# Reordering the opening of a one-core FFT filter and maxout MoE kernel: filter copies, a sine table, products, one x load, and the last transposes

## The chip, the cores and the metric

The kernel runs on one core of one Trainium2 chip. The metric is the device time of one execution in microseconds (us), as the median of several; lower is better. The core has five engines that matter here: TensorE (PE in the profile; its weight loads are PEld), VectorE (DVE), ScalarE (ACT), GpSimd (POOL) and SyncE (SP). SP does nothing but issue DMA transfers; POOL issues some too. All transfers are carried by the core's 16 DMA engines.

## The reference

The input x has 8 batches of 3072 rows with 256 columns. Along the 3072 rows each batch is filtered in the frequency domain; then every row goes through a maxout layer.

```
X = np.fft.rfft(x, axis=1)                  # x: 8 x 3072 x 256
Y = X * (filt_r + 1j * filt_i)[None]        # filter: 1537 x 256
y = np.fft.irfft(Y, n=3072, axis=1)
g = np.maximum(y @ w1, y @ w2)              # w1, w2: 256 x 1024
out = g @ w_out                             # w_out: 1024 x 256
```

## The kernel before

**The factorization.** The transform over 3072 = 96 × 32 points is done as matrix products with small tables of sines. Stage 1 transforms over 96 points (table C1), stage 2 over the 32 that are left, with one table per frequency group (U, made of arguments `ua` by a Sin on ScalarE in two halves, `sines_u(0)` and `sines_u(1)`, L247 on); then the product with the filter F; stage 3 goes back over 32 (tables VP and VQ, which `table_v` and `put_v` make out of U, L256 to L280); stage 4 goes back over 96 (table G1, made by `table_g`, L251). The maxout is written as relu(y (w1 − w2)) w_out + y M with M = w2 w_out, so the weights are prepared once: Wd = w1 − w2 by `prep_wd`, M by `prep_t` and `prep_m`.

**The steady part.** Batches 1 to 7 pass through DRAM between the stages. The main loop has 64 tiles `tt` of 384 rows, each with 8 steps: `moe_h` (y times Wd, L482) and `moe_o` (the second product with Wo, L536, of the tile before). Between them the stages of the following batches are slotted in: two lists, `todo` and `mid`, name the step at which a piece of work is put. The order of instructions on every engine is the order of the program text; each engine runs its own list in order and waits by semaphores where it needs another's result or a buffer.

**The opening.** Batch 0 is done on the chip without DRAM, before the first tile, and this is where the change lies. In order:

- `s1t(c)` and `t1(n)` (L554 to L575): stage 1 and transposes into bt[0]. ScalarE and VectorE evict alternately.
- `s2(0, v)` (L379), v = 0 to 5: four groups of columns each, half s = 0 in one PSUM tile and s = 1 in another, `px`.
- `products(v)` (L657): for each half one `product` (L388) of 128 × 1024 elements with the filter. VectorE reads px from PSUM. GpSimd does the half s = 1 of v in `POOLED` = (0, 2, 3, 4), out of a copy in SBUF that ScalarE makes in `stage_x(v)` (L650); for v = 5 `shared_product` (L394) splits that half between both.
- `s3t(v)` (L577): one matmul on a table of ones as a filler (L581; two for v = 1), then 32 matmuls in pairs (L587), and evictions into the tile zT, one per g, by ScalarE (L597), or for v >= 4 and g = 1 by VectorE (L595).
- `t2(c)` (L599): transposes of a piece of zT into zr[0] (L608), evicted by VectorE or ScalarE or both.
- `s4(tt)` (L454): stage 4 for one tile, y evicted by ScalarE and VectorE.

**The filter.** F has 128 partitions: in each half g of 64, the first 32 are loaded from DRAM by GpSimd (`load_f`, L111, 16 partitions per transfer), and the other 32 are a copy of them. The copies are made by `double_f` (L124): the columns w 0 to 8 by VectorE (four `tensor_copy`, one for each g and each of real and imaginary part, L128) and w 8 to 12 by four transfers that SyncE issues (L130). `fix_f` then sets one row. Stage v reads columns 2v and 2v + 1.

**Around it in the queues.** SyncE's list has the four copies of F, then the four loads of w1 and w2 into WS (`load_w`). GpSimd's list, behind the filter loads, has: the product of v = 0, the load of batch 1's first x (`load_x(1, 0, 2)`, 384 KB, L89), the products of v = 2, 3, 4, its share of v = 5, `load_x(1, 2, 2)`, `load_wo` (w_out into Wo, L294), one `prep_wd`, two more x loads, and the rest of the preparation. On TensorE, behind the last s3t, stand `f1(1, 0)`, a filler (`spin`), `t2(0)`, `f1(1, 1)`, a filler, `s4(0)`, `f1(1, 2)`, `f1(1, 3)`, and the main loop. `f1` (L323) is stage 1 of batch 1: one matmul of x with C1 (L330) into a PSUM tile `pa`, and at once its eviction to `at`. The PSUM pool `ps` has six buffers, `pso` two.

Of the kernel before, what the change touches and what calls it, by code (L numbers as in the profile page):

```python
# [15 lines left out]
D = 256  # L16
# [11 lines left out]
def kernel(  # L28
# [95 lines left out]
    def double_f(h, g, ri, engine):  # L124
        w0, w1 = WP[h]
        o_, i_ = F[64 * g + 32:64 * g + 64, ri, w0:w1], F[64 * g:64 * g + 32, ri, w0:w1]
        if engine is V:
            V.tensor_copy(o_, i_)  # L128
        else:
            nc.sync.dma_start(out=o_, in_=i_)  # L130
# [25 lines left out]

    hv = init.tile([128, 2, 1], FP32)
# [22 lines left out]
    def table_c():  # L180
# [10 lines left out]
        S.activation(C1, uc.rearrange("p k r -> p (k r)"), AF.Sin, bias=zero[0:NP], scale=TWO_PI)  # L191

# [58 lines left out]
    def table_g():  # L251
        pg = ps.tile([96, NP], FP32, tag="ps", name="pg")
        TE.matmul(pg, C1, I128[0:NP, 0:NP], start=True, stop=True)
# [68 lines left out]

    def f1(b, c, engine):  # L323
        if c == 0:
# [3 lines left out]
        at = at_[b]  # L328
        pa = ps.tile([96, 2, D], FP32, tag="ps", name="pa")
        TE.matmul(pa, C1, xb[b, c // 2][:, 2 * (c % 2):2 * (c % 2) + 2], start=True, stop=True)  # L330
# [57 lines left out]
    def product(E, v, s, px, pool=None):  # L388
# [3 lines left out]
        return pq  # L392

    def shared_product(v, s, px, xs_, pool):  # L394
        pq = pool.tile([128, 2, 2, D], BF16, tag="pq", name="pq")
        V.tensor_tensor(pq[:, 0], px, F[:, 0, 2 * v:2 * v + 2, s], OP.mult)
        V.tensor_tensor(pq[:, 1, 0], px[:, 0], F[:, 1, 2 * v, s], OP.mult)
        G.tensor_tensor(pq[:, 1, 1], xs_[:, 1], F[:, 1, 2 * v + 1, s], OP.mult)
# [178 lines left out]
    def s3t(v, pq):  # L577
        pool, tag = (ps, "ps") if v % 2 else (pso, "po")
        pz = [pool.tile([128, 2, 2, 2, 2, NM], FP32, tag=tag, name="pt%d" % g) for g in range(2)]
        for _ in range(2 if v == 1 else 1):  # L580
            TE.matmul(pz[0].rearrange("p i s r c m -> p (i s r c m)"), W1[:, 0:128], W1, start=True, stop=True)  # L581
        for i in range(2):
            for s in range(2):
                for dc in range(2):
                    for q, tab in enumerate((VP, VQ)):
                        for g in range(2):
                            TE.matmul(pz[g][:, i, s, :, dc], pq[s][64 * g:64 * g + 64, q, i, 128 * dc:128 * dc + 128],  # L587
                                      tab[64 * g:64 * g + 64, 2 * v + i, s].rearrange("p (r m) -> p r m", r=2),
                                      start=(q == 0), stop=(q == 1))
        zv = zT.rearrange("p c m (w g) q -> p w g (c m) q", g=2)  # L590
        for g in range(2):
            o_ = zv[:, 2 * v:2 * v + 2, g]
            i_ = pz[g].rearrange("p i s r c m -> p i (c m) (s r)")
            if v >= 4 and g == 1:
                V.tensor_copy(o_, i_)  # L595
            else:
# [232 lines left out]
```

## Time and profile before

| what | value |
| --- | --- |
| three runs | 498.36, 496.78, 498.27 us (median 498.27) |
| the profiled execution | 498.64 us, its span 496.8 us |
| TensorE busy, share of the span | 483.8 us, 97% |
| VectorE, ScalarE, GpSimd busy | 335.4, 320.4, 258.7 us (68%, 64%, 52%) |
| mean granted clock of TensorE | 0.989 |
| stretch 21.30 to 24.70 us: TensorE busy, granted clock | 1.39 us, 0.50 |
| stretch 31.50 to 35.00 us: TensorE busy, granted clock | 3.50 us, 1.00 |
| first matmul of the main loop (L482) | begins at 37.73 us |

The span runs from the first to the last instruction in the trace. Only the slices of the first 40 us have TensorE below nine tenths. A line of the chain of waits has a start, a length and an instruction; a line of the timeline has start, length, engine, source line, operation, output and inputs by the program's names, shapes and count, and in brackets the idle time before it with the engine that ended it. A line of transfers has the name, the queue, the count, the size and the median time from issue to landing in us. A granted clock of 0.50 is half of TensorE's full clock.

### The profile page before, as it was taken

Reading aid. Unit: us, or ns where it says so; the run is one execution under the profiler, and the core shown is the slowest. Engines: PE = TensorE matmul, PEld = TensorE weight load, DVE = VectorE, ACT = ScalarE, POOL = GpSimd, SP = SyncE. Lnnn points to the kernel's source line nnn. Section 1 sums busy time; section 2 is a strip of 40 time slices with the busy share of each in tenths; the row PEclk is TensorE's granted clock in tenths of the full one; section 3 lists DMA queues with packets and bytes.
Section 4 is the critical chain, followed back from the end, with each engine's and each line's share of the span. In section 5 each row is a group of like instructions: output and inputs, shape, how many; then the busy total and the mean of one; then the engine's idle time right before and its main releaser. Section 6 shows DMA issues by size and latency. Waiting matters only on the chain.

```text
span 496.8 us, 14137 instructions
## 1 busy us (share of the span) xinstructions
PE 483.8 (97%) x5759; PEld 353.5 (71%) x5759; DVE 335.4 (68%) x535; ACT 320.4 (64%) x667; POOL 258.7 (52%) x342
## 2 busy tenths in 40 slices
PE   7699999999999999999999999999999999999997
PEld 3457777777777777777777777776777777777775
DVE  7886788468855688467855688457873688556542
ACT  5777478667775677576866668665766656464442
POOL 8694868318466594528646295536842212222220
PEclk9879999999999999999999999999999999999999
DMA  8989988996789867896789977897776834531112
GB/s 128 161 242 224 259 269 260 284 234 190 204 266 221 216 210 223 249 225 174 231 257 227 183 244 211 257 215 168 227 231 175 181 104 129 157 120 66 64 64 86
DMA packets 76626, 97.30 MB, mean 196 GB/s; under 512 B 7985, under 2 KB 54354, under 8 KB 75186
## 3 DMA queue, kind: packets, MB, share of 16 engines
q1 hardware_dynamic: 63218, 66.71, 52.1%
q0 software_dynamic: 13200, 29.60, 21.4%
q8 instruction: 45, 0.74, 0.7%
q14 instruction: 19, 0.16, 0.1%
q10 hardware_dynamic: 144, 0.09, 0.1%
HBM read 53.87 MB, written 47.19 MB: 203 GB/s over the span
## 4 chain that ended last, share of the span: by engine, by line
PE 92%; DMA 3%; ACT 2%; POOL 1%; issue 1%; DVE 0%; SPq 0%; POOLq 0%
PE po L536 34%; PE ph L482 33%; PE po L534 8%; PE pz L408 5%; PE pc L443 3%; PE px L384 2%; PE pa L355 2%; DMA xb<-in_x_dram 2%; DMA zr<-zd 1%; PE pt L587 1%; DMA zd<-zt 1%; PE pr L608 1%; POOL xb L89 1%; PE pt L581 1%; PE pa L330 1%
## 5 line engine op out<-in xcount | busy, mean ns | idle before, releaser
L486 ACT ACTIVATE gt<-ph 128x384 bf16<-128x384 f32 x357 | 175.7, 496 | 138.8 <-PE ph L482 136.2
L536 PE MATMUL po<-Wo,gt 128*128 128x256 bf16 x1528 | 262.7, 273 | 1.2 <-issue 1.2
L536 PEld LDWEIGHTS <-gt 128*128 128x128 bf16 x1528 | 144.7, 98 | 68.1 <-issue 13.5
L495 POOL DMA_DIRECT2D out_dram<-ot x186 | 103.1, 558 | 154.7 <-DVE ot L547 138.7
L390 DVE TENSOR_TENSOR pq<-px,F 128x1024 bf16<-128x1024 f32 x91 | 106.9, 1218 | 25.7 <-PE px L384 25.4
L484 DVE TENSOR_SCALAR gt<-ph 128x384 bf16<-128x384 f32 x155 | 83.6, 551 | 53.5 <-PE ph L482 47.1
L482 PEld LDWEIGHTS <-Wd 128*128 128x128 bf16 x1024 | 99.6, 98 | 13.7 <-issue 0.3
L104 POOL TENSOR_TENSOR xb<-XF 128x512 bf16<-128x512 f32 x48 | 61.3, 1277 | 66.9 <-DMA XF<-in_x_dram 31.7
L547 DVE TENSOR_SCALAR ot<-po 128x512 f32<-128x512 f32 x83 | 57.0, 686 | 35.0 <-PE po L536 33.1
L105 POOL TENSOR_TENSOR xb<-XF 128x512 bf16<-128x512 f32 x48 | 61.1, 1274 | 0.0
L359 ACT ACTIVATE at<-pa 128x512 bf16<-128x512 f32 x96 | 51.8, 611 | 3.4 <-PE pa L355 3.3
L412 ACT ACTIVATE zt<-pz 128x512 bf16<-128x512 f32 x84 | 45.6, 594 | 5.7 <-PE pz L408 1.9
L448 ACT ACTIVATE ce<-pc 128x384 f32<-128x384 f32 x56 | 23.7, 490 | 6.7 <-PE pc L443 6.0
L408 PE MATMUL pz<-pq,VP 64*64 64x256 bf16 x336 | 22.2, 281 | 0.0
L384 PE MATMUL px<-bt,U 64*64 64x256 bf16 x384 | 20.4, 283 | 1.2 <-ACT VQ L279 0.7
L408 PE MATMUL pz<-pq,VQ 64*64 64x256 bf16 x336 | 21.1, 269 | 0.0
L408 PEld LDWEIGHTS <-VP 64*64 64x64 bf16 x336 | 10.0, 105 | 13.3 <-issue 12.7
L355 PE MATMUL pa<-xb,CT 64*64 64x512 bf16 x192 | 18.0, 377 | 0.0
L443 PEld LDWEIGHTS <-zr 48*128 48x128 bf16 x896 | 13.1, 93 | 4.8 <-issue 4.4
L443 PE MATMUL pc<-G,zr 48*128 48x48 bf16 x896 | 15.4, 180 | 0.3 <-DMA zr<-zd 0.3
L384 PEld LDWEIGHTS <-U 64*64 64x64 bf16 x384 | 10.6, 109 | 3.9 <-issue 3.6
L618 PE MATMUL pd<-W 128*128 128x512 bf16 x28 | 9.2, 437 | 1.5 <-DVE zero L150 1.5
(383 smaller groups left out, 632.1 us busy)
## 6 DMA issues: line engine op xcount, KB each, us to landing
out_dram<-ot POOLq DMA_DIRECT2D x186, 128.0 KB, 3.8
XF<-in_x_dram SPq DMA_DIRECT2D x96, 192.0 KB
ad<-at SPq DMA_DIRECT2D x56, 192.0 KB
zd<-zt SPq DMA_DIRECT2D x42, 256.0 KB
zr<-zd SPq DMA_DIRECT2D x56, 192.0 KB
bt<-ad SPq DMA_DIRECT2D x13, 768.0 KB
WS<-in_moe_w_dram SPq DMA_DIRECT2D x4, 512.0 KB
xb<-in_x_dram POOLq DMA_DIRECT2D x8, 192.0 KB, 5.6
```

The lines of the kernel that those rows point to most:

```text
L104: G.tensor_tensor(t_[:, 0], f[:, 0], f[:, 1], OP.add)
L105: G.tensor_tensor(t_[:, 1], f[:, 0], f[:, 1], OP.subtract)
L359: S.activation(at[:, m0:m0 + 2], pa[g], AF.Copy)
L390: E.tensor_tensor(pq, px.rearrange("p (o i) d -> p o i d", o=1).to_broadcast([128, 2, 2, D]), F[:, :, 2 * v:2 * v + 2, s], OP.mult)
L408: TE.matmul(pz[g][64 * s:64 * s + 64, i], tab[64 * g:64 * g + 64, 2 * v + i, s], pq[s][64 * g:64 * g + 64, q, i], start=(q == 0), stop=(q ...
L412: S.activation(zt[:, :, g], pz[g], AF.Copy)
L482: TE.matmul(ph, Wd[:, dc, 128 * j:128 * j + 128], y_[:, dc], start=(dc == 0), stop=(dc == 1))
L484: V.tensor_scalar(gt[tt][:, j], ph, 0.0, None, OP.max)
L486: S.activation(gt[tt][:, j], ph, AF.Relu)
L495: E.dma_start(out=dst, in_=ot[tt // 2][:, 3 * (tt % 2) + c])
L536: TE.matmul(p_, g_[:, n - 2, blk], Wo[:, n - 2], start=(e == 0), stop=(e == 9))
L547: V.tensor_scalar(ot[tt // 2][:, e - 1:e + 1], po[q // 2 % 2], SCALE, None, OP.mult)
```

## The change

All of it is in the opening.

- `double_f` takes a range of columns. SyncE copies w 4 to 8 of g = 1 (two transfers) and then w 8 to 12 of both g (four), six transfers instead of four. VectorE copies w 0 to 8 of g = 0 and w 0 to 4 of g = 1.
- `sines_u(1)` is put ahead of the t1 loop; it stood behind `stage_x(2)`. `table_v(1, 0)` follows `table_v(0, 0)`; `put_v(1, 0)` and `table_v(1, 1)` with its `put_v` stand one place earlier too.
- `shared_product` goes. GpSimd takes half s = 1 of v = 0, 2, 3 and 5 whole; VectorE takes both halves of v = 1 and 4. `stage_x(4)` is no longer needed.
- `load_x(1, 0, 2)` is issued behind the product of v = 3, GpSimd's third; it stood behind the first.
- zT has another order of its dimensions: rows in eight groups `o` of four first, partitions of the transposed piece as (g, w, q). To match, G1 is made from a second sine table, CP, whose columns have that order. For v = 5 the eviction is in two parts, the first of the eight groups alone and then the seven others, so that `t2(0)`, which reads the first group, depends on the first part.
- `f1` is split into `f1_in` (the matmul) and `f1_out` (the eviction and, every second time, the store). The matmuls of `f1(1, 0 to 3)` stay near t2(0) and s4(0); the evictions come behind s4(0), the last two in step 0 of the main loop. The fillers write one tile `pd` of the pool pso, and there are two more of them behind s4(0).

```diff
@@ -121,8 +121,7 @@
                     o_ = F[64 * g + r0:64 * g + r0 + 16, ri, w0:w1].rearrange("p w s d -> p (w s) d")
                     G.dma_start(out=o_[:, n0:n], in_=src)
 
-    def double_f(h, g, ri, engine):
-        w0, w1 = WP[h]
+    def double_f(w0, w1, g, ri, engine):
         o_, i_ = F[64 * g + 32:64 * g + 64, ri, w0:w1], F[64 * g:64 * g + 32, ri, w0:w1]
         if engine is V:
             V.tensor_copy(o_, i_)
@@ -154,6 +153,7 @@
     jb = init.tile([128, 16], FP32)
     cid = init.tile([128, 128], FP32)
 
+    CP = init.tile([NP, 96], BF16)
     hv = init.tile([128, 2, 1], FP32)
     load_x(0, 0, 1)
     G.iota(pid, pattern=[[1, 1]], base=0, channel_multiplier=1, allow_small_or_imprecise_dtypes=True)
@@ -189,6 +189,8 @@
         V.tensor_scalar(rc, uc, RND, RND, OP.add, OP.subtract)
         V.tensor_tensor(uc, uc, rc, OP.subtract)
         S.activation(C1, uc.rearrange("p k r -> p (k r)"), AF.Sin, bias=zero[0:NP], scale=TWO_PI)
+        S.activation(CP.rearrange("p (g w c) -> p g w c", g=2, c=4),
+                     uc.rearrange("p (w g s) r -> p g w (s r)", g=2, s=2), AF.Sin, bias=zero[0:NP], scale=TWO_PI)
 
     def table_ct():
         G.memset(CT, 0.0)
@@ -250,7 +252,7 @@
 
     def table_g():
         pg = ps.tile([96, NP], FP32, tag="ps", name="pg")
-        TE.matmul(pg, C1, I128[0:NP, 0:NP], start=True, stop=True)
+        TE.matmul(pg, CP, I128[0:NP, 0:NP], start=True, stop=True)
         S.activation(G1, pg, AF.Copy)
 
     def table_v(h, q):
@@ -320,14 +322,22 @@
     zd = {}
     at_ = {}
 
+    pas = {}
+
     def f1(b, c, engine):
+        f1_in(b, c)
+        f1_out(b, c, engine)
+
+    def f1_in(b, c):
+        pas[c] = ps.tile([96, 2, D], FP32, tag="ps", name="pa")
+        TE.matmul(pas[c], C1, xb[b, c // 2][:, 2 * (c % 2):2 * (c % 2) + 2], start=True, stop=True)
+
+    def f1_out(b, c, engine):
         if c == 0:
             ad[b] = dram.tile([96, NM, D], BF16, tag="ad", name="ad")
         if c % 4 == 0:
             at_[b] = apool.tile([128, 8, D], BF16, tag="at", name="at")
-        at = at_[b]
-        pa = ps.tile([96, 2, D], FP32, tag="ps", name="pa")
-        TE.matmul(pa, C1, xb[b, c // 2][:, 2 * (c % 2):2 * (c % 2) + 2], start=True, stop=True)
+        at, pa = at_[b], pas.pop(c)
         o_ = at[0:96, 2 * (c % 4):2 * (c % 4) + 2]
         if engine is V:
             V.tensor_copy(o_, pa)
@@ -389,13 +399,6 @@
         pq = (pool or pqpool).tile([128, 2, 2, D], BF16, tag="pq", name="pq")
         E.tensor_tensor(pq, px.rearrange("p (o i) d -> p o i d", o=1).to_broadcast([128, 2, 2, D]),
                         F[:, :, 2 * v:2 * v + 2, s], OP.mult)
-        return pq
-
-    def shared_product(v, s, px, xs_, pool):
-        pq = pool.tile([128, 2, 2, D], BF16, tag="pq", name="pq")
-        V.tensor_tensor(pq[:, 0], px, F[:, 0, 2 * v:2 * v + 2, s], OP.mult)
-        V.tensor_tensor(pq[:, 1, 0], px[:, 0], F[:, 1, 2 * v, s], OP.mult)
-        G.tensor_tensor(pq[:, 1, 1], xs_[:, 1], F[:, 1, 2 * v + 1, s], OP.mult)
         return pq
 
     def s3(b, v, pq):
@@ -576,25 +579,26 @@
 
     def s3t(v, pq):
         pool, tag = (ps, "ps") if v % 2 else (pso, "po")
-        pz = [pool.tile([128, 2, 2, 2, 2, NM], FP32, tag=tag, name="pt%d" % g) for g in range(2)]
+        pz = [pool.tile([128, 8, 2, 2, 2, 2, 4], FP32, tag=tag, name="pt%d" % g) for g in range(2)]
         for _ in range(2 if v == 1 else 1):
-            TE.matmul(pz[0].rearrange("p i s r c m -> p (i s r c m)"), W1[:, 0:128], W1, start=True, stop=True)
+            TE.matmul(pz[0].rearrange("p o i s r c m -> p (o i s r c m)"), W1[:, 0:128], W1, start=True, stop=True)
         for i in range(2):
             for s in range(2):
                 for dc in range(2):
                     for q, tab in enumerate((VP, VQ)):
                         for g in range(2):
-                            TE.matmul(pz[g][:, i, s, :, dc], pq[s][64 * g:64 * g + 64, q, i, 128 * dc:128 * dc + 128],
-                                      tab[64 * g:64 * g + 64, 2 * v + i, s].rearrange("p (r m) -> p r m", r=2),
+                            TE.matmul(pz[g][:, :, i, s, :, dc].rearrange("p o r m -> p r o m"),
+                                      pq[s][64 * g:64 * g + 64, q, i, 128 * dc:128 * dc + 128],
+                                      tab[64 * g:64 * g + 64, 2 * v + i, s].rearrange("p (r o m) -> p r o m", r=2, m=4),
                                       start=(q == 0), stop=(q == 1))
-        zv = zT.rearrange("p c m (w g) q -> p w g (c m) q", g=2)
-        for g in range(2):
-            o_ = zv[:, 2 * v:2 * v + 2, g]
-            i_ = pz[g].rearrange("p i s r c m -> p i (c m) (s r)")
-            if v >= 4 and g == 1:
-                V.tensor_copy(o_, i_)
-            else:
-                S.activation(o_, i_, AF.Copy)
+        for o0, o1 in ((0, 1), (1, 8)) if v == 5 else ((0, 8),):
+            for g in range(2):
+                o_ = zT[:, o0:o1, :, :, g, 2 * v:2 * v + 2].rearrange("p o c m w q -> p o (c m) (w q)")
+                i_ = pz[g][:, o0:o1].rearrange("p o i s r c m -> p o (c m) (i s r)")
+                if v >= 4 and g == 1:
+                    V.tensor_copy(o_, i_)
+                else:
+                    S.activation(o_, i_, AF.Copy)
 
     def t2(c, engines):
         if c == 0:
@@ -605,7 +609,8 @@
             m0 = 4 * c + n * k
             for m in range(n):
                 for dc in range(2):
-                    TE.transpose(pr[:, m, 128 * dc:128 * dc + 128], zT[:, dc, m0 + m].rearrange("p u q -> p (u q)"),
+                    TE.transpose(pr[:, m, 128 * dc:128 * dc + 128],
+                                 zT[:, (m0 + m) // 4, dc, (m0 + m) % 4].rearrange("p g w q -> p (g w q)"),
                                  I128)
             if engine is V:
                 V.tensor_copy(zr[0][:, m0:m0 + n], pr)
@@ -622,9 +627,10 @@
     V.tensor_scalar(I128, cid, pid, None, OP.is_equal)
     V.tensor_scalar(NI, cid, pid, -1.0, OP.is_equal, OP.mult)
     tables_u()
-    for g in range(2):
-        for ri in range(2):
-            double_f(1, g, ri, nc.sync)
+    for w0, w1 in ((4, 8), (8, 12)):
+        for g in range(w0 == 4, 2):
+            for ri in range(2):
+                double_f(w0, w1, g, ri, nc.sync)
     for h in range(2):
         load_w(h)
     spin(12)
@@ -637,13 +643,15 @@
         if c < 7:
             spin(2)
     bt[0] = bpool.tile([128, NU, D], BF16, tag="bt", name="bt")
-    zT = bpool.tile([128, 2, NM, NU, 4], BF16, tag="bt", name="zT")
+    zT = bpool.tile([128, 8, 2, 4, 2, NW, 4], BF16, tag="bt", name="zT")
+    sines_u(1)
     for n in range(6):
         t1(n, S if n % 2 else V)
     put_v(0, 0, table_v(0, 0))
+    pv1 = table_v(1, 0)
     for g in range(2):
         for ri in range(2):
-            double_f(0, g, ri, V)
+            double_f(0, 4 if g else 8, g, ri, V)
     fix_f()
     xs = {}
 
@@ -652,36 +660,30 @@
         S.activation(t_, pxs[v][1], AF.Copy)
         xs[v] = t_
 
-    POOLED = (0, 2, 3, 4)
+    POOLED = (0, 2, 3, 5)
 
     def products(v):
         pool = pq0 if v > 2 else pqpool
         pq = [product(V, v, 0, pxs[v][0], pool)]
-        if v == 5:
-            pq.append(shared_product(v, 1, pxs[v][1], xs[v], pool))
-        else:
-            pq.append(product(G, v, 1, xs[v], pool) if v in POOLED else product(V, v, 1, pxs[v][1], pool))
+        pq.append(product(G, v, 1, xs[v], pool) if v in POOLED else product(V, v, 1, pxs[v][1], pool))
         return pq
 
     pqs = {}
     pxs = {v: s2(0, v) for v in (1, 0)}
     stage_x(0)
     put_v(0, 1, table_v(0, 1))
+    put_v(1, 0, pv1)
     pxs[2] = s2(0, 2)
     stage_x(2)
-    sines_u(1)
-    put_v(1, 0, table_v(1, 0))
+    put_v(1, 1, table_v(1, 1))
     pxs[3] = s2(0, 3)
     stage_x(3)
-    put_v(1, 1, table_v(1, 1))
     for v in (1, 0, 2):
         pqs[v] = products(v)
-        if v == 0:
-            load_x(1, 0, 2)
     s3t(1, pqs[1])
     pxs[4] = s2(0, 4)
-    stage_x(4)
     pqs[3] = products(3)
+    load_x(1, 0, 2)
     s3t(0, pqs[0])
     pxs[5] = s2(0, 5)
     stage_x(5)
@@ -708,14 +710,23 @@
     ypool = ctx.enter_context(tc.tile_pool(name="ypool", bufs=7))
     cepool = ctx.enter_context(tc.tile_pool(name="cepool", bufs=3))
     gpool = ctx.enter_context(tc.tile_pool(name="gpool", bufs=2))
-    f1(1, 0, S)
-    spin(1)
+    pd = pso.tile([128, 512], FP32, tag="po", name="pd")
+
+    def fill(n):
+        for _ in range(n):
+            TE.matmul(pd, W1[:, 0:128], W1, start=True, stop=True)
+
+    f1_in(1, 0)
+    fill(1)
     t2(0, (V, S))
-    f1(1, 1, V)
-    spin(1)
+    f1_in(1, 1)
+    f1_in(1, 2)
+    fill(1)
     s4(0)
-    f1(1, 2, S)
-    f1(1, 3, V)
+    f1_in(1, 3)
+    f1_out(1, 0, S)
+    f1_out(1, 1, V)
+    fill(2)
 
 
     todo = {}
@@ -752,6 +763,8 @@
     plan(0, 9, prep_m)
     for c, n in ((2, 7), (4, 22), (5, 32), (6, 40), (7, 48)):
         plan(0, n, t2, c, (V,))
+    plan(0, 0, f1_out, 1, 2, S)
+    plan(0, 0, f1_out, 1, 3, V)
     plan_f1(0, 1, (5, 6, 7, 7, 9, 9, 10, 10, 11, 11, 12, 12), 13)
     plan_f2(0, (25, 28, 31, 35, 38, 42, 46), ((0,), (), (1,), (2,), (3,), (4,), (5, 6)),
             (8, 8, 10, 12, 17, 20, 24, 28), (10, 13, 16, 20, 24, 27, 30, 33))
```

## The prediction

> **What bounds the kernel now.** I read the page's slices first, then the chain of waits, then the opening stretch by stretch.
>
> Busy tenths and granted clock over the span, one digit per 12.4 us:
>
> ```profile
> PE   7699999999999999999999999999999999999997
> PEclk9879999999999999999999999999999999999999
> ```
>
> TensorE is full from the fourth slice to the last, and the change leaves that work alone. It can only move the moment at which the stream of L482 and L536 begins (the first L482 is at 37.73 us), or a landing that this stream waits for. So the whole case lies in 18 to 46 us.
>
> The chain of waits there (start, us, what):
>
> ```profile
> 23.07 0.83 ACT U L249
> 23.95 0.59 PE pv L265 x19
> ...
> 34.11 0.62 PE pt L587 x32
> 34.76 0.70 DVE zT L595
> 35.59 0.63 PE pr L608 x8
> ```
>
> The sines hold the inverse tables (PE idle 1.5 us). Behind them the chain is TensorE's own until the last zT eviction, then t2. But the first s3t waits for its products; their engines:
>
> ```profile
> 18.49 4.76 DVE L128 COPY F<-F 32x4096 bf16<-32x4096 bf16 x4
> 23.76 8.13 DVE L390 TENSOR_TENSOR pq<-px,F 128x1024 bf16<-128x1024 f32 x7 [0.19 <-DVE F L145]
> ...
> 23.43 2.12 POOL L390 TENSOR_TENSOR pq<-xs,F 128x1024 bf16<-128x1024 f32 x1 [1.20 <-DVE F L128]
> 25.50 0.56 POOL L89 DMA_DIRECT2D xb<-in_x_dram  x1
> 26.07 6.30 POOL L390 TENSOR_TENSOR pq<-xs,F 128x1024 bf16<-128x1024 f32 x3
> ...
> 32.95 0.56 POOL L89 DMA_DIRECT2D xb<-in_x_dram  x1
> 33.51 0.93 POOL L294 DMA_DIRECT2D Wo<-in_moe_w_out_dram  x1
> ```
>
> DVE is packed from the copies to 32.8, POOL from 23.4 on. The transfers (stretches from 25.0, 32.5 and 35.0; last column us from issue to landing):
>
> ```profile
> xb<-in_x_dram POOLq DMA_DIRECT2D x1, 384.0 KB, 6.2
> ...
> Wo<-in_moe_w_out_dram POOLq DMA_DIRECT2D x1, 512.0 KB, 10.6
> xb<-in_x_dram POOLq DMA_DIRECT2D x1, 384.0 KB, 6.8
> ...
> xb<-in_x_dram POOLq DMA_DIRECT2D x2, 384.0 KB, 11.0
> ```
>
> The two of 35 us, behind Wo in POOL's queue, took 10.06 and 11.85. The next batch's first x landed at 25.50 + 6.25 = 31.75, 2.87 us before its first use (f1 at 34.62). Wo landed at 33.51 + 10.56 = 44.07, and is first used at 44.19:
>
> ```profile
> 34.62 0.42 PE L330 MATMUL pa<-xb,C 96*96 96x512 bf16 x1
> ...
> 44.19 0.60 PE L536 MATMUL po<-Wo,gt 128*128 128x256 bf16 x4
> ```
>
> Two slacks then: 2.87 us on x, 0.12 us on Wo, whatever the engines do. By stretches (us, PE, PEld, DVE, ACT, POOL, clock, DMA share, GB/s):
>
> ```profile
> 21.30:24.70 3.40, 1.39 (x39) 0.69 (x38) 3.18 (x4) 2.40 (x6) 2.20 (x2) 0.50 0.70 146
> 28.10:31.50 3.40, 3.29 (x60) 1.53 (x54) 3.37 (x4) 2.90 (x6) 3.40 (x3) 0.50 1.05 289
> 31.50:35.00 3.50, 3.50 (x131) 2.37 (x125) 2.25 (x5) 3.00 (x7) 3.50 (x5) 1.00 1.03 321
> ```
>
> The DMA engines are full from 28 us, the clock is half in 21.29 to 31.53; s3t's 32 matmuls last 0.97 us there and 0.57 after.
>
> **The change part by part.**
>
> *Filter copies.* DVE's four copies of 4096 elements (1.22 us, one each 1.14) become two of 4096 and two of 2048: 2 × 1.14 + 2 × 0.64 = 3.56 for 4.76, so products start at 22.55 instead of 23.76, 1.2 us earlier. SP gains two transfers of 128 KB. They wait for the g=1 parts, landed 18.54 and 20.26, and took 2.3 to 3.6 us for SP's others: landed by about 22.3 and 23.8. Their first reader is the product of v=2, DVE's fourth, at 27.17: 3 us of cover. SP's other doubles wait for parts landing to 24.46 anyway, so WS (issued 25.07) stays queued where it was. The 256 KB cost the filter loads between nothing (share 0.70: room) and 256 KB at 190 GB/s = 1.35 us; I take nothing and keep 1.35.
>
> *Sines.* 0.83 us on ACT move to between the last at eviction (ends 15.08) and the first bt eviction (16.43); that gap is 1.34 us. Cost nothing; if ua came late bt would slip, but DVE finished it at 13.5. PE loses its 1.5 us wait at L265. ACT's put_v and stage_x shift forward by 0.8: the staging of v=3 ends 24.9, before 25.88. The new small Sin for CP (96×96, 0.38 us) falls into 1.8 us of ACT idle near 4.3 us: nothing; that table_g takes CP changes only the order of columns. table_v(1,0), 24 matmuls in 0.59 us, moves ahead of the first px; those wait for the last bt eviction (19.28) anyway, and TensorE idles again until 24.9 (1.39 busy of 3.40 in the stretch from 21.3): nothing.
>
> *Products.* POOL does v 0, 2, 3, 5 whole; DVE eight whole ones: 22.55 + 8 × 1.13 + 0.1 = 31.8, before 32.82. POOL: v0 22.25 to 24.37, v2 to 26.44, v3 to 28.52, then the x issue, v5 from its staging (30.63) to 32.8 (33.0 before). Thus Wo issues near 33.3, 0.2 earlier.
>
> *TensorE.* The first s3t starts when v=1's products are done: 24.91, before 25.95 (the spins ahead of it began 25.97). All six s3t then go about 1 us earlier; the last ends near 33.95 (34.70 before, some 0.3 of the gain lost as s3t(2) still runs at half clock). zT's last eviction in parts lets t2(0) start after an eighth: an eviction of 512 elements costs 0.69 on DVE, one of 64 lies between 0.2 and 0.28 (the 256-element cast); saves 0.4. Alone this puts t2(0) at 34.25, before 35.59: 1.3 us won.
>
> *The x load.* Now issued behind v3, at 28.48, 2.98 later, past two products in POOL's queue. At 6.25 it lands at 34.73; the slack of 2.87 turns to a wait, as f1's first matmul stands ahead of t2(0) in TensorE's order. Bounds: 2 stretches of 384 KB at the 160 GB/s half share of the 321 = 2.4 us of moving plus the 2.3 us that the quickest 128 KB double took, 33.2; the later loads' 10.06 gives 38.5. I take 6.25, the nearest in size, queue and company; 6.81, the next one, gives 35.3. So f1 34.78, one fill, t2(0) 35.2: 0.4 us won of 1.3.
>
> The Trainium skill (DMA: Bandwidth & Descriptors, Anatomy of one DMA — SWDGE (gpsimd) path) gives a fixed 2.0 us and bytes over 436 GB/s. By that estimate x takes 2.9 us, lands at 31.4 and binds nothing, and the sum would be the 1.3 us. The trace disagrees: 6.25 to 11.85 us for this size.
>
> *f1 split.* Evictions of four pa are moved behind s4: two on each of ACT (0.61) and DVE (0.69). From t2(0) to the first L482 stays 2.17 us; the two fills there (0.21 each) lie in the wait for y's evictions. But DVE now does f1 1 and 3 just ahead of its gt and of zr for t2(1), which moves from +4.22 to +4.62 after t2(0)'s start, and py(1) waits for it some 0.37: bounds 0 and 0.7 (one f1 eviction); 0.2 to 0.4 us of loss. Net of all: 0.0 to −0.2 us.
>
> *Behind it.* An earlier stream meets Wo. Its landing is set by the DMA engines: the slowest carries WS to 36.58, x to 39.76, Wo to 44.07 without a gap. With unchanged bytes in that run Wo lands where it did, and no gain beyond 0.12 + 0.2 = 0.3 us passes L536. Bound above: other engines had their Wo shares by 40.1 to 43.25, so up to 1.3 if the slowest is relieved.
>
> Sum: −0.2 for t2(0) and its follow-ups, within the cap of 0.3. The profiled execution took 498.64 (span 496.8 plus 1.84 around it), so 498.4 for it; it stands 0.37 above the median of 498.27, which gives 498.05, and 0.3% (1.5 us) is what a measurement here can tell.
>
> **The rivals.**
>
> *A: both late loads are quick (faster).* The x load, issued at 28.48, meets the end of WS instead of its start and lands by 33.2 to 33.8; then s3t alone sets t2(0), at 34.25 (−1.3), or at 33.7 (−1.9) if the half clock also ends a window of 3.4 us earlier, at 28.1, where s3t(0), px5 and s3t(2) would win 0.4 + 0.35 + 0.4. And the engine that held Wo is relieved by the 1.3 us, so that the cap is 0.3 + 1.3 = 1.6. For it: s3t begins 1 us earlier, so the window from 24.7 is fuller than its 3.10 of 3.40. Against: no load of this size took under 6.25, and Wo's cap needs a second piece of luck. Decides from x at 33.8 with Wo at 42.6; time −1.6, 496.7, down to −2.2 with the y work shorter by the 0.35 that I charged: 496.1.
>
> *B: the x load takes longer (slower).* It is put into a full stretch (share 1.05) where WS's 2 MB are queued, while it had been issued into 0.56. From 8.4 us on it lands after 36.9, t2(0) at 37.4 or later; at 10.06, 38.5. For it: the loads got slower in issue order (6.25, 6.81, 10.06, 11.85). Against: the last two had Wo's 512 KB ahead in their own queue, and this one has none. Decides from 7.0 us on; with 8.4 to 10, +1.8 to +3.4: 500.5.
>
> The Trainium skill (the same page, Issuing engines are not separate DMA queues) says that transfers of all issuers share the 16 engines, which leaves a move to SP's queue saving only issue time. That would make the next case likelier; no row separates it yet.
>
> *C: SP's extra 256 KB delay the filter.* All later F parts land up to 1.35 us later; the x issue and the products slip by 0.9, t2(0) 36.1: +0.5, inside "same".
>
> *D: the reordering doesn't act:* TensorE was slowed by its own half clock, not by the products, and s3t keeps its pace: within ±0.3 of before.
>
> **How the numbers follow.** Forecast 0.34, C 0.06, D 0.06, A 0.29, B 0.25. Within 0.3%: 0.34 + 0.06 + 0.06 = 0.46, and 0.02 of B, x only just over 7 us: 0.48. Faster 0.29; slower 0.23. The likeliest time is 498.0 (497.4 to 498.9 by itself, for an x load of 5.6 to 7.1 us). The range goes from A's far end, 496.1, to 500.3, past which lies some half of B (0.12).
>
> **What would show it.** Right: DVE's copies take 3.5 us, the first L587 is at 25.9, L249 no longer stops L265, the x load is issued at 28.5 and lands near 34.7; L330 is followed by t2(0) near 35.2; L536 first at 44.0 with a wait for Wo. Wrong (faster): x lands by 33.9 and L536 at 43 without a wait; the clock is 1.0 before 31.5. Wrong (slower): x lands after 36, or new waits at L460 over 0.7 us.

## The result: slower, and the profile after

Six runs of the changed kernel have a median of 502.12 us (500.16 to 502.85), six of the kernel before, taken with them, 497.63 us (496.65 to 498.36). The ratio is 1.0085, with a 95% interval of 1.0063 to 1.0108: about 4.2 us slower, outside the range and on the side of rival B. The profiled execution took 502.85 us, its span is 501.1.

The slices of the page, busy tenths and granted clock: the loss shows in the third digit of PE (9 before, 5 now) and in the fourth of PEclk (9 before, 7 now). The 7 at the end of PE stands in both kernels.

```profile
PE   7759999999999999999999999999999999999997
PEclk9877999999999999999999999999999999999999
```

The chain of waits of the changed kernel (start, us, what) no longer goes through the zT evictions. It goes through the x load:

```profile
27.76 1.38 issue
29.13 9.14 DMA xb<-in_x_dram
38.31 0.66 PE pa L333
39.40 0.85 PE pr L612 x8
```

The timeline of the engines ahead of it (start, us, engine, line, shapes, count, idle before):

```profile
19.01 3.70 DVE L127 COPY F<-F 32x4096 bf16<-32x4096 bf16 x4
23.20 9.14 DVE L400 TENSOR_TENSOR pq<-px,F 128x1024 bf16<-128x1024 f32 x8 [0.19 <-DVE F L144]
...
22.88 6.30 POOL L400 TENSOR_TENSOR pq<-xs,F 128x1024 bf16<-128x1024 f32 x3 [1.37 <-DVE F L127]
29.13 0.56 POOL L89 DMA_DIRECT2D xb<-in_x_dram  x1
31.04 2.13 POOL L400 TENSOR_TENSOR pq<-xs,F 128x1024 bf16<-128x1024 f32 x1 [1.34 <-ACT xs L660]
...
25.90 0.58 SPq L289 DMA_DIRECT2D WS<-in_moe_w_dram  x1
...
27.58 0.90 SPq L290 DMA_DIRECT2D WS<-in_moe_w_dram  x1
```

The copies are 1.06 us shorter and the products start sooner (7.55 us after the first t1 transpose; 8.62 before), as forecast. But x is issued at 29.13, after the last of WS's four loads, where it had been issued beside the first. What the engines carried while the x load waited, 29.6 to 33.0 us (queue, kind: packets, MB, share of 16 engines):

```profile
DMA packets 563, 1.10 MB, mean 322 GB/s; under 512 B 28, under 2 KB 28, under 8 KB 563
...
q1 hardware_dynamic: 563, 1.10, 97.2%
...
xb<-in_x_dram POOLq DMA_DIRECT2D x1, 384.0 KB, 9.1
```

All 563 packets are of SyncE's queue (q1). GpSimd's (q0) moved none until 33.2 us, 4.1 us after the issue. TensorE meanwhile (stretches with PE, PEld, DVE, ACT, POOL busy, clock, DMA share, GB/s; then its timeline):

```profile
31.50:35.00 3.50, 2.07 (x97) 1.65 (x96) 2.30 (x4) 2.88 (x7) 3.50 (x4) 1.00 1.06 310
35.00:38.40 3.40, 0.09 (x1) 0.09 (x2) 0.00 (x0) 0.00 (x0) 3.40 (x5) 0.63 1.04 186
38.40:42.00 3.60, 3.60 (x22) 2.33 (x23) 0.42 (x1) 0.65 (x2) 3.60 (x4) 0.50 1.27 182
```

```profile
38.31 0.66 PE L333 MATMUL pa<-xb,C 96*96 96x512 bf16 x1 [4.49 <-DMA xb<-in_x_dram]
...
42.97 0.81 PE L485 MATMUL ph<-y__996,Wd 128*128 128x384 bf16 x4
...
49.46 0.60 PE L539 MATMUL po<-Wo,gt 128*128 128x256 bf16 x4
```

An idle stretch of 4.49 us, and with it the half clock, from 35.85 to 42.68 us: from t2(0), at 39.20, to the first L485 it takes 3.77 us where it took 2.14 before (35.59 to 37.73). The account between the two profiled executions: the first t1 transpose starts 0.51 later (15.65 and 15.14; in all the profiles below it lies between 14.58 and 16.00, with nothing of the change ahead of it but one small Sin in an idle stretch), t2(0) is 3.08 later against that start, the stretch from t2(0) to the first L485 is 1.63 longer, and the first L539 is 5.27 late. The stream keeps 5.3 us of delay until 320 us; then about a microsecond of it goes, because this one execution of before had stalls of 0.28 and 1.23 us at 326 and 335 us, where the other had one of 0.59. Nothing of the change lies there; so the spans differ by 4.3.

### The profile page after: what moved, and what is told of

It reads as the page before. It is cut to its first block, busy times and chain, and to the rows that moved or that the text cites. A ratio compares the mean times of both kernels' runs of the same rounds, so it can differ in the third digit from the quotient of the medians.

```text
span 501.1 us, 14143 instructions
## 1 busy us (share of the span) xinstructions
PE 484.6 (97%) x5757; PEld 354.8 (71%) x5761; DVE 334.6 (67%) x535; ACT 320.4 (64%) x668; POOL 257.1 (51%) x341
## 4 chain that ended last, share of the span: by engine, by line
PE 92%; DMA 4%; ACT 1%; POOL 1%; issue 1%; POOLq 0%; DVE 0%
PE po L539 35%; PE ph L485 33%; PE po L537 8%; PE pz L411 5%; DMA xb<-in_x_dram 4%; PE pc L446 3%; PE pa L365 2%; PE px L394 2%; PE pa L333 1%; PE pr L612 1%; POOL xb L89 1%; PE py L463 1%; ACT bt L576 0%; PE pm__1158 L314 0%; ACT VQ L281 0%
## 5 line engine op out<-in xcount | busy, mean ns | idle before, releaser
L539 PE MATMUL po<-Wo,gt 128*128 128x256 bf16 x1528 | 262.5, 273 | 0.0
L539 PEld LDWEIGHTS <-gt 128*128 128x128 bf16 x1528 | 144.7, 98 | 67.4 <-issue 12.8
L400 DVE TENSOR_TENSOR pq<-px,F 128x1024 bf16<-128x1024 f32 x92 | 108.0, 1219 | 25.7 <-PE px L394 25.4
L485 PEld LDWEIGHTS <-Wd 128*128 128x128 bf16 x1024 | 99.6, 98 | 13.4 <-POOL CT L196 0.2
L616 DVE COPY zr<-pr 96x1024 bf16<-96x1024 bf16 (+1 forms) x8 | 5.2, 650 | 9.8 <-PE pr L612 9.8
```

The lines of the kernel that those rows point to most:

```text
L400: E.tensor_tensor(pq, px.rearrange("p (o i) d -> p o i d", o=1).to_broadcast([128, 2, 2, D]), F[:, :, 2 * v:2 * v + 2, s], OP.mult)
L485: TE.matmul(ph, Wd[:, dc, 128 * j:128 * j + 128], y_[:, dc], start=(dc == 0), stop=(dc == 1))
L539: TE.matmul(p_, g_[:, n - 2, blk], Wo[:, n - 2], start=(e == 0), stop=(e == 9))
```

## The experiments

My theory when the result was known, called W in the expectations: the whole loss comes from the x load, which the move put behind WS's 2 MB. The rivals: the other parts cost too (P), SyncE's two more copies slow every load (S).

Since single executions start up to 1.4 us apart, I read the experiments' traces by the time from the first t1 transpose (L573; L570 in the kernel before).

### x_back: the move of the x load undone

```diff
     for v in (1, 0, 2):
         pqs[v] = products(v)
+        if v == 0:
+            load_x(1, 0, 2)
...
     pqs[3] = products(3)
-    load_x(1, 0, 2)
```

> The changed kernel with one edit undone: load_x(1, 0, 2) is issued behind GpSimd's first product again. Theory W (the x load was queued behind the 2 MB of WS, because it was moved past WS's issues, and everything else in the change is a small gain): x is issued near 25.0, ahead of WS, lands by 31 to 32.5, the first f1 matmul follows the last s3t with no wait near 34.5 to 35.2 (GpSimd's products slip by 0.6 us), the first L485 at 36.5 to 37.3, the clock stays 1.0 from 35 on; time 0.5 to 1.5 us under before, 496.1 to 497.1. Rival P (the split of f1, the extra copies on SyncE and the other parts cost too): still slower than before by 1 us or more, over 498.6, with new waits behind t2(0). Rival S (SyncE's 256 KB more delay every load): x takes 8 us or more even from 25.0 and lands after 33.

Measured: 498.52 us, ratio 1.0005 (0.9987 to 1.0023). The loss is gone with this one edit, and P falls as an explanation of it; S too: issued at 25.30, the load took 5.0 us. But the gain of the rest that I expected isn't there: t2(0) comes 0.67 us sooner than before, measured from the first t1 transpose, and the first L539 0.25. The timeline of x_back shows why t2(0) gained only half of the forecast 1.3 us; its last two lines are the load and what the engines carried from 26.5 to 29.1 us:

```profile
23.55 5.75 DVE L400 TENSOR_TENSOR pq<-px,F 128x1024 bf16<-128x1024 f32 x5 [0.19 <-DVE F L144]
31.17 3.49 DVE L400 TENSOR_TENSOR pq<-px,F 128x1024 bf16<-128x1024 f32 x3 [1.86 <-DMA F<-F]
...
25.30 0.56 POOL L89 DMA_DIRECT2D xb<-in_x_dram  x1
...
xb<-in_x_dram POOLq DMA_DIRECT2D x1, 384.0 KB, 5.0
...
q0 software_dynamic: 86, 0.35, 97.1%
```

VectorE's product of v = 4 waits 1.86 us for SyncE's last copy of F, issued at 26.02 and landed at 30.95. The x load went ahead of that copy on the engines: between 26.5 and 29.1 only GpSimd's packets move.

### x_late_only: the move alone, in the kernel before

```diff
     for v in (1, 0, 2):
         pqs[v] = products(v)
-        if v == 0:
-            load_x(1, 0, 2)
...
     pqs[3] = products(3)
+    load_x(1, 0, 2)
```

> The kernel before with one edit: load_x(1, 0, 2) is issued behind GpSimd's third product. Theory W: WS is issued from 25.07 as before, the x load near 29.6 stands behind it, moves nothing until WS is nearly through (33 to 35) and lands at 37.5 to 39.5; the first f1 matmul waits for it some 3 to 4.5 us, TensorE's clock falls to half behind the idle stretch, and the time is 3.5 to 5.5 us over before, 501.1 to 503.1, the whole of the change's loss or more. Rival P: the load is at most a part of it, under 2 us slower than before.

Measured: 500.60 us, ratio 1.0060 (1.0038 to 1.0082): the move by itself is 3 us slower, most of the whole loss, though under the 3.5 to 5.5 that I wrote. The load and the matmul that waits for it:

```profile
30.00 0.56 POOL L89 DMA_DIRECT2D xb<-in_x_dram  x1
...
xb<-in_x_dram POOLq DMA_DIRECT2D x1, 384.0 KB, 7.3
...
37.31 0.42 PE L330 MATMUL pa<-xb,C 96*96 96x512 bf16 x1 [2.54 <-DMA xb<-in_x_dram]
```

It landed 7.3 us after its issue, less than I wrote, and the half clock behind it lasted 3.4 us (38.39 to 41.80), half as long as in the changed kernel. The wait is shorter than in the changed kernel for one more reason: here s3t ends about 1 us later, so TensorE has less time to wait.

### ws_after_x: the same place, nothing queued ahead

```diff
     load_x(1, 0, 2)
+    seen = dram.tile([1, 256], BF16, tag="seen", name="seen")
+    nc.sync.dma_start(out=seen, in_=xb[1, 0][0:1, 0])
+    for h in range(2):
+        load_w(h)
```

The two lines of `load_w` near the start are taken out.

> The changed kernel with WS's four loads on SyncE behind a small store that reads the first x tile, so that WS is issued only when x has landed. It measures how long the x load, issued at the same place in GpSimd's list (29.1), takes with nothing queued ahead of it. Theory W: its first packet moves 2 to 2.5 us after the issue and it lands in 4 to 6 us, by 33 to 35, against 9.14 in the changed kernel, with s3t, products and staging as they were. Rival S or a slow load for another reason (GpSimd being idle or VectorE's products beside it): it takes 8 us or more here too. The time says nothing on this: WS lands some 6 us later, the preparation of Wd with it, and the kernel is slower than the changed one by 0 to 8 us.

Measured, the load's time to landing and the issues:

```profile
xb<-in_x_dram POOLq DMA_DIRECT2D x1, 384.0 KB, 5.1
...
29.05 0.56 POOL L89 DMA_DIRECT2D xb<-in_x_dram  x1
...
34.18 0.23 SPq L686 DMA_DIRECT2D seen<-xb  x1
```

5.1 us instead of 9.14, from the same place (29.05 and 29.13), with the same products, copies and staging around it. Its first packet moved 1.3 us after the issue (30.3 us), where the changed kernel's moved after 4.1. So WS in front of it is what made the load long. f1 starts at 34.22 and t2(0) 19.17 us after the first t1 transpose, against 20.46 before: the 1.3 us that the early products were to bring are real, where x doesn't stand in the way. The time, 508.08, says nothing, as WS is late.

The Trainium skill (DMA: Bandwidth & Descriptors, Anatomy of one DMA — SWDGE (gpsimd) path) would give 2.9 us for 384 KB as an estimate. Here it took 5.11 us with nothing ahead, and the quickest load of this size in all the traces took 4.53 (the second x load of this run).

The Trainium skill (the same page, Queues, rings and completion order) says that each DMA engine goes round-robin between the queues it has work for, packet by packet. The 563 to 0 packets above don't look like that: the load's first packets came as if there were one queue in the order of issue. Once it moves, the two queues do share the engines. In the kernel before, where the load and WS were issued together, both moved from 28.2 to 31.0 us:

```profile
q0 software_dynamic: 106, 0.37, 66.6%
q1 hardware_dynamic: 187, 0.36, 35.0%
```

What holds the first packets back, no run here shows.

### x_second: half the move

```diff
-    load_x(1, 0, 2)
...
     for v in (1, 0, 2):
         pqs[v] = products(v)
+    load_x(1, 0, 2)
```

> The changed kernel with load_x(1, 0, 2) behind GpSimd's second product, near 27.1, in the middle between the old and the new place. By then all six copies of F and two or three of WS's four loads are issued. Theory W (what counts is the order against WS, as the engines hardly take the load's packets while WS's are queued): it still lands at 35 to 38, 8 to 10 us after its issue, TensorE waits, and the time is 1.003 to 1.008 of before; VectorE's product of v = 4 waits for no copy of F. If only the lateness of the issue counts (5 to 6.3 us each time), it lands by 33.5, TensorE waits for nothing, and the time is 0.996 to 1.000 of before.

Measured: 498.41 us, ratio 1.0006 (0.9984 to 1.0029), so the time is not what W gave. The profile is:

```profile
27.69 0.56 POOL L89 DMA_DIRECT2D xb<-in_x_dram  x1
...
36.20 0.66 PE L333 MATMUL pa<-xb,C 96*96 96x512 bf16 x1 [2.74 <-DMA xb<-in_x_dram]
```

8.5 us, issued between WS's third and fourth load. But that profiled execution took 500.43, the longest of ten; four of the ten took 496.8 to 497.2. The three longest have a mean granted clock of 0.986 to 0.990, the other seven 0.992 or 0.993, so the half clock that follows a long wait is likely in those three alone. I take it that the load is in a race between WS's issues, which the profile lost and the quick runs won. As these have no profile, and the kernel before spread from 496.4 to 501.1 in the same set, that is argued, not shown.

### warm_wait: the wait without the half clock

```diff
+    fill(16)
     f1_in(1, 0)
     fill(1)
     t2(0, (V, S))
```

> The changed kernel with 16 more filler matmuls of 0.21 us on TensorE ahead of the first f1 matmul, which is where it waits for x. They take 3.4 of the 4.5 idle us, and change no transfer. If the half clock behind the wait (35 to 41.8 us) is a cost of its own, the clock stays 1.0, the stretch from t2(0) to the first L485 falls from 3.8 to 2.2 us, and the time is 1.2 to 1.8 us under the changed kernel: 500.3 to 500.9. If the half clock costs nothing (the stretch is bound by the evictions), or falls for another reason, it is the changed kernel's time within 0.5 us. The x load lands at 38 in both.

Measured: 499.78 us, ratio 1.0036 (1.0020 to 1.0051). Against the changed kernel's 1.0085 that is some 2.4 us less, with the two ratios' intervals apart, for work that computes nothing. The stretches and TensorE's timeline:

```profile
35.00:38.40 3.40, 3.40 (x17) 1.56 (x16) 0.76 (x2) 0.62 (x2) 1.89 (x3) 1.00 1.04 302
```

```profile
34.87 3.63 PE L717 MATMUL pd<-W 128*128 128x512 bf16 x16
38.33 0.38 PE L333 MATMUL pa<-xb,C 96*96 96x512 bf16 x1
...
40.98 0.87 PE L485 MATMUL ph<-y__1012,Wd 128*128 128x384 bf16 x4
```

The clock stays at 1.00 and t2(0) to L485 takes 2.21 us. So of the loss, 1.6 us (3.77 − 2.21) were the half clock behind the idle stretch, by the trace. Counted from f1's first matmul, which the half clock slows too, it is 2.0 (38.31 to 42.97 in the changed kernel, 38.33 to 40.98 here). The other executions agree: their mean granted clock is 0.992 to 0.995 in all eight here, and 0.985 to 0.989 in all six of the changed kernel.

Two reservations on the 2.4 us of the times. In this execution, the longest of the eight, x landed 6.25 us after its issue, at 35.25, as SyncE had issued WS's last two loads only after it. For the same reason TensorE then waited 1.00 us for Wd, at 43.94. How the load fared in the other seven isn't known.

### f1_later and combo: the reader moved instead

```diff
-    f1_in(1, 0)
     fill(1)
     t2(0, (V, S))
-    f1_in(1, 1)
-    f1_in(1, 2)
-    fill(1)
+    fill(3)
     s4(0)
-    f1_in(1, 3)
-    f1_out(1, 0, S)
-    f1_out(1, 1, V)
-    fill(2)
+    fill(3)
...
+    for c, n in ((0, 2), (1, 3), (2, 3), (3, 4)):
+        plan(0, n, f1, 1, c, S if c % 2 == 0 else V)
```

The two planned f1_out go. combo has this, and

```diff
     prep_wd(0, G)
+    prep_wd(1, G)
     for c in (4, 6):
         load_x(1, c, 2)
-    for q in range(1, 4):
+    for q in range(2, 4):
         prep_wd(q, G)
```

> The changed kernel with the x load left where the change put it, but its reader moved: the matmuls and evictions of f1(1, 0 to 3) go into steps 2, 3, 3 and 4 of the main loop, and filler matmuls take their places. Theory W (the loss is TensorE's wait for x, and the half clock that follows the idle stretch): x lands near 38 as before the edit, nothing waits for it, t2(0) starts near 34.5, the first L485 near 36.7, and the time falls by 3.5 to 5.5 us from the changed kernel's ratio of 1.0085: to between 0.998 and 1.002 of before. It is not lower, because the preparation of Wd on GpSimd (second quarter done near 38.1) and the landing of w_out then hold the stream. Rival (something else of the change holds the stream, the split evictions or the products): still 1.004 or more.

> f1_later with one more edit: GpSimd makes the second quarter of Wd ahead of the two x loads instead of behind them, 1.06 us earlier, so that the third L485 doesn't wait for it. If Wd is what holds the stream in f1_later, the first L539 comes 0.5 to 1 us earlier than there, and the time is 0.997 to 1.000 of before; if WS's own landing (37 to 38) or w_out's holds it, it is the same as f1_later within 0.3 us.

Measured: f1_later 498.80 us, ratio 1.0025 (0.9993 to 1.0057); combo 497.65 us, ratio 1.0008 (0.9978 to 1.0039). The wait for x is gone and most of the loss with it, as W says; but neither is quicker than before, and both spread: eight of twelve runs of f1_later took 496.6 to 499.2 us, four 501.1 to 503.3; of combo eight took 495.9 to 497.9 and four 501.5 to 502.9. The profiled execution of combo is one of the longer ones (501.46). In its timeline:

```profile
42.56 0.50 PE L485 MATMUL ph<-y__992,Wd 128*128 128x384 bf16 x2 [2.62 <-POOL Wd L300]
...
30.48 3.49 DVE L400 TENSOR_TENSOR pq<-px,F 128x1024 bf16<-128x1024 f32 x3 [2.23 <-DMA F<-F]
```

There SyncE's third issue of WS took 1.50 us instead of 0.5, the x load was issued ahead of the fourth, and WS landed at 41.11 instead of 37.41: then Wd is late instead of x, and the half clock follows that wait too (42.97 to 46.39). The four longest runs of combo all have a mean granted clock of 0.990, the other eight 0.992 to 0.997; that those lost the same way is likely, not shown. Both orders on the engines cost something; the kernel before has x where neither waits.

### back4 and sines_only: what the early parts bring

back4 is x_back with the copies of F as before:

```diff
-    for w0, w1 in ((4, 8), (8, 12)):
-        for g in range(w0 == 4, 2):
-            for ri in range(2):
-                double_f(w0, w1, g, ri, nc.sync)
+    for g in range(2):
+        for ri in range(2):
+            double_f(8, 12, g, ri, nc.sync)
...
-            double_f(0, 4 if g else 8, g, ri, V)
+            double_f(0, 8, g, ri, V)
```

sines_only is the kernel before with

```diff
+    sines_u(1)
     for n in range(6):
         t1(n, S if n % 2 else V)
...
     stage_x(2)
-    sines_u(1)
```

> x_back with one more edit undone: the copies of F as before (four by SyncE, four whole ones by VectorE). In x_back VectorE waited 1.86 us for SyncE's last copy of F, which was issued at 26.02 and came behind the x load on the engines (landed 30.95), and the early start of the products was lost there. If moving copies to SyncE makes that race (its six copies take the place in its queue), then with four the last copy lands before VectorE's fifth product, VectorE doesn't wait, products begin 1.1 us later and end no later than in x_back, and the time is within 0.3% of before, 0.998 to 1.001. If the last filter load's own landing sets it (25.3 to 26.5 in the runs with six copies, 24.5 to 25.5 with four), the wait for F can stand here too, and nothing changes against x_back (1.0005).

> The kernel before with one edit: sines_u(1) ahead of the t1 loop. TensorE's wait of 1.5 us at L265 goes, but the first s3t waits for VectorE's two products of v = 1, which wait for the copies of F, so it begins 11.6 to 11.9 us after the first t1 transpose, as before (11.80), and t2(0) 20.2 to 20.6 after it (20.46). If the tables held the chain, as the chain of waits shows it, both come 0.8 to 1.5 us earlier. Its one time can't tell, 496.5 to 499.

Measured: back4 498.44 us, ratio 1.0005 (0.9987 to 1.0023). VectorE's products begin later (8.62 us after the first t1 transpose; 7.55 in x_back) and at v = 4 they wait 0.21 us where x_back waits 1.86 (the last copy of F has landed at 30.01, before that product), and t2(0) starts 19.23 us after that transpose (x_back 19.79, before 20.46). Yet the first L539 comes at 29.13 us after it, where it came at 29.05 before. What took the 1.2 us back, in the list of waits of back4 (us in total, times, longest) and its timeline:

```profile
PEld L485 <- POOL Wd L300: 1.6, 3, 0.8
...
39.00 0.44 PEld L485 LDWEIGHTS <-Wd 128*128 128x128 bf16 x4 [0.55 <-POOL Wd L300]
40.22 0.11 PEld L485 LDWEIGHTS <-Wd 128*128 128x128 bf16 x2 [0.78 <-POOL Wd L300]
```

It is GpSimd's preparation of Wd. The 1.6 us are waits of the weight loads. TensorE's own matmuls came some 1.1 us late by the two shown: 3.27 us from the first L485 to the second tile's L463 (37.29 to 40.56), where the kernel before took 2.15. Wd stands behind GpSimd's whole product of v = 5, and the change hardly brings that product forward (it ends 18.1 us after the first transpose in back4 and 17.65 in x_back; before, GpSimd's quarter ended at 17.9). In f1_later the weight loads wait 1.0 us for Wd, in x_back 0.3.

sines_only took 498.48 us in its one run. TensorE's first s3t began 10.05 us after the first transpose, 1.75 earlier than before, which I had denied: its first matmuls need only one of v = 1's two products. It ended 1.0 earlier, but by the fourth s3t the gain was gone, with the clock at 0.76 over 31.5 to 35.0 us where it had been 1.00, and t2(0) came at 20.56, against 20.46. So in this one execution the wait for the sines, which stood in the chain of before, wasn't worth its 1.5 us.

### combo2, back_wd and best1: three tries to keep the gain

combo2 is combo with the x load behind GpSimd's last product and f1 later in the main loop (0 to 3 at steps 4, 5, 5, 6, the others at 8 to 13, the read of bt at 14 instead of 13):

```diff
-    load_x(1, 2, 2)
+    load_x(1, 0, 2)
     load_wo()
...
-    for c in (4, 6):
+    for c in (2, 4, 6):
         load_x(1, c, 2)
```

back_wd is x_back and best1 is f1_later with the x load as in combo2, both with

```diff
     t2(0, (V, S))
+    prep_wd(1, V)
```

and GpSimd making the other three quarters; best1 also has the last two x loads behind them, f1(1, 0 to 3) at steps 5, 5, 6, 6, and the others at 9 to 12.

> combo with the x load issued behind GpSimd's last product (near 32.7, ahead of w_out), so that all of WS is on the engines before it in every run, and with f1(1, ...) later in the main loop: 0 to 3 at steps 4, 5, 5, 6, the others at 8 to 13 and the read at 14. combo and f1_later fell into two groups (combo 495.9 to 497.9 and 501.5 to 502.9); in combo's slow profile the x load's packets went ahead of WS's last ones, WS landed at 41.1 and TensorE waited 2.62 us for Wd. Theory W: with the order WS before x fixed, the slow group goes, WS lands by 36 to 37.5 and the time is 0.996 to 0.999 of before. If the two groups come from something else (the copies of F landing 2 us late), they stay, and the ratio is 1.000 or more.

> x_back (ratio 1.0005) with one more edit: the second quarter of Wd is made by VectorE behind t2(0)'s eviction, where VectorE idled 0.97 us, instead of by GpSimd behind two x loads, so that GpSimd's third and fourth quarter and the casts come 1.24 us earlier. Theory D (with the x load in its old place the change does bring t2(0) forward by 0.7 to 1.2 us, measured from the first t1 transpose, but GpSimd's preparation of Wd, which the change leaves or makes later, takes it back at L485): no wait for Wd at L485 is left, the first L539 comes 27.8 to 28.4 us after the first t1 transpose instead of 28.8 to 29.1, and the time is 0.996 to 0.9995 of before. Rival: what takes the gain back is something else (the landing of w_out or the last copy of F): 1.000 to 1.002 and L539 at 28.8 to 29.2.

> f1_later with the x load behind GpSimd's last product (as in combo2, where no run fell into a slow group and WS landed at 35.3), the second quarter of Wd on VectorE behind t2(0), GpSimd's third and fourth quarter ahead of the last two x loads, f1(1, 0 to 3) at steps 5, 5, 6, 6, the others at 9 to 12, the read at 13. Theory W and D together: no wait for x, Wd or bt; t2(0) 19.0 to 19.2 us after the first t1 transpose, L539 at 27.5 to 28.3 after it instead of 29.05; time 0.996 to 0.999 of before, and no group 4 us above. If the load of w_out, now between the x loads, or f1's evictions hold the stream, it is 1.000 or more.

Measured: combo2 499.95 us, ratio 1.0042 (1.0025 to 1.0058). Its seven runs lie closer together (499.1 to 501.5) and WS landed at 35.3, as expected, but it waits in two new places that the edit itself made: 1.5 us for Wd, which stands behind three x loads on GpSimd, and, at 62.9 us, for the later read:

```profile
PE px L394 <- DMA bt<-ad: 1.4, 1, 1.4
```

back_wd: 498.93 us, ratio 1.0010 (0.9986 to 1.0033); its profiled execution was the second longest of its twelve (504.29), so its trace isn't used, and the time decides neither for nor against theory D. best1: 498.94 us, ratio 1.0010 (0.9985 to 1.0034). No wait for Wd is left in best1's list, and its first L539 comes 28.67 us after the first transpose, 0.4 sooner than before. But VectorE lost 2.10 us to the last copy of F again, and the read of bt made TensorE wait 1.46 us. None of the versions is quicker than the kernel before.

## Why the prediction was wrong

**The step that failed** is the x load: "At 6.25 it lands at 34.73", taken as "the nearest in size, queue and company". It took 9.14. The company was not the same: at 25.50 the load was issued beside WS's first, at 29.13 behind all four, and the runs show that this order is what counts: 4.8 to 5.1 us ahead of WS (back4, x_back, ws_after_x), 6.25 to 8.5 among its four issues (before, warm_wait, sines_only, combo, x_second), 7.3 to 9.1 up to 2.2 us behind the last (x_late_only, f1_later, the changed kernel), and 6.4 to 6.5 at 3 to 5 us behind it (combo2, best1). The row that I quoted for the later loads, 10.06 us, was the nearer one, and so was my own sentence that the engines are full from 28 us. I read the issue-to-landing time as a property of the transfer; of these 9.1 us, 4.0 were the queue ahead of it (5.1 with nothing ahead).

**Rival B** named the place and the sign ("It is put into a full stretch (share 1.05) where WS's 2 MB are queued"), at a chance of a quarter. My argument against it, that the slow loads had w_out ahead in their own queue, fell: what lies ahead on the other queue does the same.

**The price left out.** B's +1.8 to +3.4 had the wait and no clock. A stretch of 4.49 us without work brought TensorE 6.8 us of half clock, another 1.6 us behind t2(0) and 0.4 ahead of it. The top of the range was 2.0 us above the median of before. By the trace the 3.08 us at t2(0) pass that already, and the 1.6 come on top.

**The steps that held.** Copies: 3.70 us for a forecast 3.56. SyncE's two new ones landed at 22.26 and 23.13 (22.3 and 23.8). The first s3t began at 26.40, 10.74 us after the first t1 transpose where it was 11.80 before: 1.06 us, as worked out. s3t ended 1.4 us earlier by the same measure, more than the forecast 0.75, with the half clock over at 29.03 instead of 31.53, as A had thought possible; in ws_after_x, where it lasted to 31.40, s3t ended 0.8 earlier. t2(0) would have started 1.3 us earlier, which ws_after_x shows. The sines cost nothing in the gap.

**The caps.** Of what would hold an earlier stream I named w_out's landing. It landed at 43.02 in the changed kernel and at 42.51 in x_back, 6.4 and 2.3 us before its first use, and held nothing. In back4 it landed at 44.65, 0.32 us before its first use: there it would have been the next to hold the stream. What did hold it is Wd, on GpSimd (1.1 us in back4), which the prediction doesn't name. And the last copy of F: I gave it cover "anyway", but the products now come a microsecond sooner, and in four of the nine profiles with six copies that I read it landed four or more us after its issue and VectorE waited 1.9 to 2.2 us. In x_back the x load stood ahead of it; in warm_wait, combo and best1 it didn't, and what held it there is open.

## What to carry to other kernels

When a load is moved, look at what has been issued on every queue by its new place, not only on its own: its duration in the old trace belongs to the old place. Price a long wait on TensorE with the slower clock behind it: here waits of 2.54 (x_late_only), 2.62 (combo), 2.74 (x_second) and 4.49 us brought 3.4 to 6.8 us of half clock, and waits of 1.00 (warm_wait) and 1.47 (combo2) none. And before counting a gain on the critical chain, list the next two or three things due just behind it with their slack; here x had 2.87 us, F's last copy 2.6 (landed 26.78, first used 29.42), Wd 0.3 (third quarter done 39.23, used at 39.55), and each of them took the gain in one of the versions.

## What I had not expected of the hardware

A load that was issued behind another queue's loads moved nothing for long: 3.4 us with 563 packets of SyncE's queue and none of GpSimd's (the changed kernel; 1.3 us from issue to first packet with nothing ahead), and 2.6 us the other way round (x_back, where one copy of F waited). Issued together, the two queues shared the engines (106 and 187 packets in 2.8 us, before). Sixteen matmuls whose result nobody reads made the kernel about 2.4 us faster (1.0085 to 1.0036). How much of that is the clock and how much a shorter wait in some executions stays open; the one trace gives 1.6 to 2.0 us to the clock.
